# Query loads of six batches moved from the sync engine's DMA queue to GpSimd's, with a third buffer

**Chip, cores, metric.** One core of a Trainium2 chip. Times are device microseconds of a run; a profile's span, from the first to the last instruction, is one to four us shorter. PE is TensorE, DVE VectorE, ACT ScalarE, POOL GpSimd, SP the sync engine; "SPq" and "POOLq" are their queues.

## The reference

Retention over 8 batches, 8 heads, 576 tokens, head size 64, then a gated unit with a causal convolution of 5 taps. All float32 in and out.

```python
scores = scale * np.matmul(q, k.transpose(0, 1, 3, 2))
ret = scores * Dmat[None]                 # Dmat[h,i,j] = gamma_h ** (i - j) for i >= j, else 0
attn = np.matmul(ret, v)
x = attn.transpose(0, 2, 1, 3).reshape(B, S, H * D)
gate_pre = sum(conv_w[k] * xp[:, k:k + S, :] for k in range(5))    # xp: x padded in front
out = (sigmoid(gate_pre) * (x @ w_val)) @ w_out
```

## The kernel before

A batch is four chunks of 128 tokens and a tail of 64; two tails share a chunk, which makes 36 chunks. A software pipeline runs over steps t, one chunk each: keys and values are loaded six steps ahead, cast to bf16 by GpSimd, and the keys are transposed by PE. Queries come as one load of 1 MB per batch. Every second step starts a gated unit of two chunks (convolution, value product, output projection).

```python
def load_queries(b):
    t = half.tile([P, H, RQ, D], F32, name="fqb", bufs=2)
    nc.sync.dma_start(out=t.rearrange("p h r d -> p h (r d)"), in_=q[b, ...])   # 1 MB, rows of 1 KB
# ... loads ahead of the loop, sync queue:
#     k0 q(batch 0) v0 k1 v1  w_val  k2 v2  w_out  k3 v3  q(batch 1)  k4 v4 k5 v5
def prep_wo(copy, o):
    copy(wob[:, o], wof[:, o])            # output weights, f32 -> bf16, 128x512
# ...
for b in range(2, B):
    first = min(s for s in qjobs if ("batch", b, 0) in qjobs[s])
    qload.setdefault(max(0, first - LA + 2), []).append(b)     # LA = 8
# in step t, cut:
    for b in qload.get(t, []):
        load_queries(b)
    if t >= 0 and ok(t + LA - 2): load(t + LA - 2)
    if ok(t + 2): cast_v(t + 2)                                # GpSimd
    if ok(t + 3): cast_k(t + 3)                                # GpSimd from chunk 2 on
    for job in qjobs.get(t + 1, []): cast_q(job)               # GpSimd
    # ... PE: scores, values, conv, transposes, projection
    if t == 2:
        for o in range(NP):
            prep_wo(s_copy if o % 2 else v_copy, o)            # two casts on ACT, two on DVE
```

## Time and profile before

| | before |
|---|---|
| median of the first 3 runs | 177.81 us (176.45 to 177.91) |
| the profiled run | 180.25 us, which counts as slow (over 1.5% above the fastest run); span 177.4 us |
| PE / DVE / ACT / POOL busy | 86 / 66 / 50 / 46% |
| share of the DMA engines, sync queue | 90.9% |

A share of busy time says who has little slack, not who sets the end.

### The profile page before, as it was taken

Reading aid. Unit: us, or ns where it says so; the run is one execution under the profiler, and the core shown is the slowest. Engines: PE = TensorE matmul, PEld = TensorE weight load, DVE = VectorE, ACT = ScalarE, POOL = GpSimd, SP = SyncE. Lnnn points to the kernel's source line nnn. Section 1 sums busy time; section 2 is a strip of 40 time slices with the busy share of each in tenths; the row PEclk is TensorE's granted clock in tenths of the full one; section 3 lists DMA queues with packets and bytes.
Section 4 is the critical chain, followed back from the end, with each engine's and each line's share of the span. In section 5 each row is a group of like instructions: output and inputs, shape, how many; then the busy total and the mean of one; then the engine's idle time right before and its main releaser. Section 6 shows DMA issues by size and latency. Waiting matters only on the chain.

```text
span 177.4 us, 5549 instructions
## 1 busy us (share of the span) xinstructions
PE 151.7 (86%) x2273; PEld 112.2 (63%) x2273; DVE 117.7 (66%) x229; ACT 88.4 (50%) x180; POOL 81.6 (46%) x119
## 2 busy tenths in 40 slices
PE   0166359398999999999999969999999999999980
PEld 0055147247786868677786848686777868677640
DVE  6558724366867777877867747777778678876430
ACT  6351412345565565557554545655575654455231
POOL 5165135492942494631386058524775662620000
PEclk9999999969999999999999999999999999999998
DMA  5999999999999899989999979999989998853114
GB/s 126 292 280 247 220 291 211 296 294 206 266 262 256 207 271 213 251 209 235 249 247 285 287 181 245 292 207 215 288 228 224 276 251 180 203 213 123 51 68 118
DMA packets 93958, 40.20 MB, mean 227 GB/s; under 512 B 80090, under 2 KB 88302, under 8 KB 93934
## 3 DMA queue, kind: packets, MB, share of 16 engines
q1 hardware_dynamic: 93744, 39.59, 90.9%
q8 instruction: 17, 0.28, 0.7%
q10 hardware_dynamic: 190, 0.27, 0.6%
q14 instruction: 7, 0.06, 0.1%
HBM read 30.42 MB, written 9.44 MB: 225 GB/s over the span
## 4 chain that ended last, share of the span: by engine, by line
PE 74%; DMA 9%; SPq 8%; DVE 2%; POOL 2%; ACT 1%; issue 1%; ACTq 0%; DVEq 0%; POOLq 0%
PE g L391 17%; PE g L380 17%; PE g L365 12%; PE tps L222 10%; DMA fkc<-in_k_dram 9%; PE o L301 6%; PE s L260 6%; SPq L78 4%; PE st L332 4%; SPq L110 3%; PE o L284 3%; POOL kb L197 1%; DVE z L383 1%; ACT qtb L244 1%; ACT ob L394 1%
## 5 line engine op out<-in xcount | busy, mean ns | idle before, releaser
L269 DVE TENSOR_TENSOR p<-s,maskq 128x512 bf16<-128x512 f32 x64 | 43.9, 685 | 15.6 <-PE s L260 15.4
L197 POOL CAST kb<-fkc 128x512 bf16<-128x512 f32 x34 | 20.8, 611 | 50.4 <-DMA fkc<-in_k_dram 38.0
L202 POOL TENSOR_TENSOR vb<-fvc,gin 128x512 bf16<-128x512 f32 x36 | 37.6, 1044 | 12.6 <-DMA fvc<-in_v_dram 9.0
L383 DVE TENSOR_TENSOR z<-gate,g 128x512 bf16<-128x512 f32 x36 | 24.8, 688 | 20.4 <-PE g L380 20.4
L391 PE MATMUL g<-wob,z 128*128 128x512 bf16 x144 | 37.5, 389 | 0.3 <-DVE z L383 0.3
L380 PE MATMUL g<-xg,wvb 128*128 128x256 bf16 x288 | 36.9, 274 | 0.0
L394 ACT COPY ob<-g 128x512 f32<-128x512 f32 x36 | 21.1, 586 | 28.9 <-PE g L391 28.6
L373 ACT ACTIVATE gate<-g 128x512 f32<-128x512 f32 x36 | 19.5, 594 | 20.0 <-PE g L365 20.0
L380 PEld LDWEIGHTS <-wvb 128*128 128x128 bf16 x288 | 26.8, 98 | 3.5 <-issue 0.8
L343 ACT CAST sbd<-st 64x256 bf16<-64x256 f32 x48 | 17.6, 366 | 16.2 <-PE st L332 15.7
L222 PE MATMUL tps<-ident,kb 128*128 128x128 bf16 x144 | 15.1, 231 | 12.1 <-POOL kb L197 7.5
L365 PE MATMUL g<-xg,dg 64*64 64x256 bf16 x720 | 24.3, 279 | 0.0
L215 POOL CAST qb<-fqb 128x512 bf16<-128x512 f32 x30 | 18.7, 632 | 7.1 <-DMA fqb<-in_q_dram 7.1
L311 DVE TENSOR_TENSOR xg<-o,gout 128x512 bf16<-128x512 f32 x32 | 21.8, 680 | 0.0
L230 DVE COPY kt<-tps 128x512 bf16<-128x512 bf16 x36 | 15.3, 424 | 8.5 <-PE tps L222 8.2
L365 PEld LDWEIGHTS <-dg 64*64 64x64 bf16 x720 | 19.0, 109 | 2.3 <-issue 0.6
L244 ACT COPY qtb<-tps 128x512 bf16<-128x512 bf16 x27 | 15.9, 589 | 8.7 <-PE tps L222 8.7
L391 PEld LDWEIGHTS <-z 128*128 128x128 bf16 x144 | 12.9, 100 | 11.6 <-issue 1.8
L222 PEld LDWEIGHTS <-kb 128*128 128x128 bf16 x144 | 8.8, 101 | 17.5 <-POOL kb L197 8.6
L222 PEld LDWEIGHTS <-qb 128*128 128x128 bf16 x144 | 11.3, 103 | 11.6 <-POOL qb L215 4.2
L222 PE MATMUL tps<-ident,qb 128*128 128x128 bf16 x132 | 13.0, 222 | 3.3 <-DVE kt L230 1.5
L301 PE MATMUL o<-p,vb 128*64 128x128 bf16 x288 | 15.8, 235 | 0.0
(58 smaller groups left out, 123.2 us busy)
## 6 DMA issues: line engine op xcount, KB each, us to landing
fkc<-in_k_dram SPq DMA_DIRECT2D x32, 256.0 KB, 5.3
fqb<-in_q_dram SPq DMA_DIRECT2D x8, 1024.0 KB, 7.9
fvc<-in_v_dram SPq DMA_DIRECT2D x32, 256.0 KB, 5.7
out_dram<-ob SPq DMA_DIRECT2D x32, 256.0 KB, 4.3
wvf<-in_moe_w_val_dram SPq DMA_DIRECT2D x1, 1024.0 KB, 6.5
wof<-in_moe_w_out_dram SPq DMA_DIRECT2D x4, 256.0 KB, 6.2
fkc<-in_k_dram SPq DMA_DIRECT2D x8, 128.0 KB, 3.9
fqc<-in_q_dram SPq DMA_DIRECT2D x8, 128.0 KB, 4.6
```

What stands on the lines that cost most here:

```text
L197: (nc.vector if t < 2 else nc.gpsimd).tensor_copy(kb, loaded["k", *chunks[t]])
L202: nc.gpsimd.tensor_tensor(vb, loaded["v", *chunks[t]], gin[:, chunks[t][2], :].unsqueeze(2).to_broadcast([P, H, D]), op=ALU.mult)
L222: nc.tensor.transpose(ps[:, pr, :], flat[:, pr * P:(pr + 1) * P], ident)
L269: nc.vector.tensor_tensor(p, sps[t][i], m.unsqueeze(1).to_broadcast([P, NP, P]), op=ALU.mult)
L301: nc.tensor.matmul(o[r, pr, :], lhsT=vb[:, 2 * pr + i, :], rhs=pt[t, i][:, pr, :], start=(fresh and pr == 0), stop=(pr == NP - 1), skip_gr ...
L311: nc.vector.tensor_tensor(by_token(x[:, bl, :, PAD + i0:PAD + i0 + P]), ops[t].rearrange("p o (r n) -> p o n r", r=RQ), by_token(gout[:, : ...
L365: nc.tensor.matmul(g[bank][cols, pr, :], lhsT=dg[rows, blk, kk, :], rhs=xs(n, rows, blk, kk), start=(pr == 0 and kk == 0), stop=(pr == 1 a ...
L373: nc.scalar.activation(t, gps[n][i], AF.Sigmoid)
L380: nc.tensor.matmul(vps[:, j, :], lhsT=wvb[:, o, 2 * i + j, :], rhs=xs(n, slice(0, P), o, PAD), start=(j == 0 and o == 0), stop=(j == 1 and ...
L383: nc.vector.tensor_tensor(z, gsb[n][i], vps, op=ALU.mult)
L391: nc.tensor.matmul(o, lhsT=zsb[n, j // 2][:, j % 2, i * P:(i + 1) * P], rhs=wob[:, j, :], start=(j == 0), stop=(j == NP - 1))
L394: nc.scalar.copy(ob, o)
```

## The change

The intent: take the large query loads out of the line in which keys and values stand, and give them a third buffer, so that they can be issued later. Batches 0 and 1 stay on the sync queue.

```diff
         def load_queries(b):
-            t = half.tile([P, H, RQ, D], F32, name="fqb", bufs=2)
-            nc.sync.dma_start(out=t.rearrange("p h r d -> p h (r d)"),
+            t = half.tile([P, H, RQ, D], F32, name="fqb", bufs=3)
+            (nc.sync if b < 2 else nc.gpsimd).dma_start(out=t.rearrange("p h r d -> p h (r d)"),
                               in_=q[b, :, 0:RQ * P, :].rearrange("h (p r) d -> p h (r d)", r=RQ))
@@
-            qload.setdefault(max(0, first - LA + 2), []).append(b)
+            qload.setdefault(max(0, first - LA + 4), []).append(b)
```

## The prediction

> **What bounds the kernel now.** I read the page first: busy shares and the slices.
>
> ```profile
> PE 151.7 (86%) x2273; PEld 112.2 (63%) x2273; DVE 117.7 (66%) x229; ACT 88.4 (50%) x180; POOL 81.6 (46%) x119
> ...
> PE   0166359398999999999999969999999999999980
> ...
> DMA  5999999999999899989999979999989998853114
> ...
> q1 hardware_dynamic: 93744, 39.59, 90.9%
> ```
>
> A slice is 4.4 us. PE has gaps up to about 42 us and is then full to the end; the DMA engines are full from the first slice to about 150 us. Two resources are close to their limits, so the question is which of them the end follows. The view of waits answers it, for PE over the whole span, then for 42 to 168 us alone (columns: total us, times, longest):
>
> ```profile
> PE tps L222 <- POOL kb L197: 7.5, 3, 4.9
> PE tps L222 <- DVE kb L197: 4.5, 1, 4.5
> PE g L222 <- POOL qb L215: 4.0, 1, 4.0
> ```
>
> ```profile
> PE tps L222 <- POOL kb L197: 1.4, 1, 1.4
> ```
>
> From 42 us on PE waits once, for 1.4 us (at 103 us, for a key chunk that landed late). Everything else that PE loses, it loses in the first 42 us. The chain of waits names a 9 us DMA piece before 102.8 us, but the timeline of PE shows it busy until 101.7 us or so: the chain followed GpSimd's wait, of which only 1.4 us reached PE. So in steady state the end moves only with PE, and whatever delays PE once in the start is never won back: PE does its sixteen two-chunk units from 42.2 to 167.3 us back to back, 7.8 us each.
>
> In the start the largest single gap of PE that a load decides is before the transposes of key chunk 3. The timelines show it, of the load queue, of GpSimd and of PE (start us, length, what):
>
> ```profile
> 10.70 5.56 SPq L110 DMA_DIRECT2D wof<-in_moe_w_out_dram  x4
> 16.30 0.59 SPq L78 DMA_DIRECT2D fkc<-in_k_dram  x1
> 16.94 0.58 SPq L78 DMA_DIRECT2D fvc<-in_v_dram  x1
> 17.57 3.94 SPq L94 DMA_DIRECT2D fqb<-in_q_dram  x1
> 21.55 1.43 SPq L78 DMA_DIRECT2D fkc<-in_k_dram  x1
> ...
> 28.23 1.81 SPq L94 DMA_DIRECT2D fqb<-in_q_dram  x1
> ```
>
> ```profile
> 15.97 0.61 POOL L197 CAST kb<-fkc 128x512 bf16<-128x512 f32 x1
> 17.45 1.04 POOL L202 TENSOR_TENSOR vb<-fvc,gin 128x512 bf16<-128x512 f32 x1 [0.88 <-DMA fvc<-in_v_dram]
> 23.41 0.61 POOL L197 CAST kb<-fkc 128x512 bf16<-128x512 f32 x1 [4.91 <-DMA fkc<-in_k_dram]
> ```
>
> ```profile
> 18.57 0.64 PE L301 MATMUL o<-p,vb 128*64 128x128 bf16 x8
> 24.08 0.61 PE L222 MATMUL tps<-ident,kb 128*128 128x128 bf16 x4 [4.87 <-POOL kb L197]
> ```
>
> The key load of 16.30 us is chunk 3. It lands at about 23.3 us because 1 MB of output weights and what was queued before it go first; GpSimd casts it at once; PE then starts and never again waits for a load until 103 us. The query load of 28.23 us is batch 2's, the first that the change moves. It now comes behind chunks 3, 4, 5 and batch 1's queries.
>
> **What the skill says.** "DMA: Bandwidth & Descriptors", section "Issuing engines are not separate DMA queues": transfers from the sync, scalar and GpSimd queues run on the same 16 engines and interleave; another issuer saves only its issue time. The trace agrees as far as it can: there is one full resource, and the sync queue's issues take 0.4 us when there is room and up to 3.9 us when there is not. The same page, "Queues, rings and completion order": each engine takes turns between the queues that have work, packet by packet. So a GpSimd load does not stand in line behind the sync queue's; no trace here shows it yet, as nearly all goes through one queue. The same page, "Anatomy of one DMA": about 2 us fixed per GpSimd DMA, descriptor making small but variable; no duration of that is in this trace. "SBUF — State Buffer", section "SBUF: two separate sides": a copy of VectorE in a two-port mode locks GpSimd out while it makes descriptors. VectorE's large groups here (masks, gates, x, transposed keys) all read PSUM, so I expect none of it after the start.
>
> **The change part by part.** I count the main loop's steps t (one key chunk each) by the order of instructions on each engine.
>
> 1. Bytes. None are added or removed: six loads of 1 MB change their queue. Full DMA engines stay full.
>
> 2. Time of issue. The diff moves each load two steps later in program order (batch 3 from step 1 to 3, 4 from 5 to 7, 5 from 11 to 13, 6 from 15 to 17, 7 from 19 to 21). But GpSimd's program is ahead of the sync queue's, which is held by full rings and by output stores. In the timelines the sync queue issues batches 4 to 7 at 48.1, 75.3, 92.4 and 109.6 us; GpSimd begins steps 7, 13, 17 and 21 at 48.6, 72.3, 92.5 and 109.8 us. So for these four the load leaves at nearly the same moment as before. Batch 3 goes later (32.4 to about 37 us), with its first cast about 10 us after that.
>
> 3. Batch 2 is the exception. Its step is cut off at 0 both before and after, and GpSimd reaches step 0 right after its cast of key chunk 2, at 15.97 + 0.61 = 16.6 us. The third buffer is new, so nothing holds it. The load therefore leaves at 16.6 us and not at 28.2 us: 11.6 us earlier, at the same moment as key chunk 3, and beside it and not behind it.
>
> 4. What that costs key chunk 3. In the trace's DMA records those of 1,024 bytes take 54 ns in the mean; a batch of queries is 1,024 of them, 64 for each of 16 engines, so 64 x 54 ns = 3.5 us of all engines. Until chunk 3 lands, some 5.8 us of engine time remain from 17.5 us on (16.6 plus about 1 us to the first byte, an estimate from the page). With equal turns the 3.5 us of queries fit whole into that stretch. The key lands at about 23.3 + 3.5 = 26.8 us. With a slow descriptor maker that spreads the load over 10 us it would be 5.8 / (1 - 0.35) = 8.9 us after 17.5, 26.4 us, so 3.1 us late. This delay is on the path: PE sits idle for it. Later start loads do not add: chunk 4 was ready 1.6 us before PE asked for it and moves by the same 3.5 us as PE does. **+3.5 us** at the start, kept to the end.
>
> 5. What is won. At 93.75 us chunk 21's key load is issued just behind batch 6's queries and lands 8.95 us later, PE's one late wait. Beside the queries and not behind them, and with PE later by 3.5 us, it is in time. **-1.4 us.**
>
> 6. GpSimd's time for making descriptors, say d a load. Before step 17 the key cast it delays ends at 95.6 us and PE wants it at 98.6 us; step 21: 112.9 against 115.9; step 13: 75.4 against 83.2; step 7: 51.7 against 59.3; step 3: 38.3 against 43.4. Some of these casts wait for a landing first, and PE is 2 to 3.5 us later after the change, so the nearest places bear a d of about 6 to 7 us. I expect d between 1 and 6: **0 us**.
>
> 7. Removing six issues from the sync queue, in all some 12 us of its time, helps keys and values leave earlier; PE does not wait for them anyway: **0 us**.
>
> Sum: 177.8 + 3.5 - 1.4 = **179.9 us**, 1.2% slower, within 2%.
>
> **The rivals.** (a) GpSimd becomes a bound. Speaking for it: 1,024 rows per load make many descriptors, GpSimd would block in order ahead of its casts, and if d is 10 us the places of point 6 fall short by 2 to 4 us in steps 0, 3, 17 or 21. Against: GpSimd is 46% busy, and most of its idle time is waiting for landings. It would make 182 to 187 us. (b) The early load is harmless and mixing queues makes the engines more efficient, or the load's first byte is so late that chunk 3 slips by only 1 us: then the win of point 5 remains and later query waits fall away, 176.5 to 178 us. For it: between 15 and 25 us the windows show 230 to 242 GB/s, and 294 GB/s between 10 and 15 us, so small rows leave something to gain. Against: the engines' share is already over 1 in both stretches. (c) Keys and values starve in mid-kernel: a query row of 1,024 bytes takes as many turns as a key row of 256, so for some 5 us after each query load keys get a small share, and PE waits at several places by 1 to 2 us. Against: these loads had stood wholly behind the queries until now. It would make 181 to 184 us. (d) PE's clock: it ran at half speed for 3.4 us at about 37 us after the gaps of the start; a shifted start may drop or repeat such a stretch, 1.5 us to either side.
>
> **Range and chances.** Points 4 and 5 alone, with 2.5 to 4 us and 0 to 1.4 us, make 178.9 to 181.8 us; (d) and the runs' own spread of 1.4 us widen it below, (a) and (c) above: 177.4 to 183.6 us. Over 2% faster (below 174.3) would need a start that gets shorter, for which I see no mechanism: 0.03. Over 2% slower (above 181.4) takes (a), (c) or an unlucky clock: 0.25. The rest, 0.72.
>
> **What would show each step.** Right if the first query issue on GpSimd's queue stands at 16 to 18 us, the cast of key chunk 3 begins at 26 to 27 us and not at 23.4, PE's longest wait for it grows from 4.9 to about 8 us, PE's first output projection of steady state shifts by the same, and the wait at 103 us is gone. Wrong in point 3 or 4 if chunk 3's cast stays near 23.4 us; wrong in 6 if PE waits for key casts at steps 3, 13, 17 or 21 with GpSimd's queue occupied before them; wrong as a whole if PE between 45 and 168 us is no longer full, for then the end would follow the DMA engines or GpSimd.

## The result, and the profile after

The changed kernel takes **185.11 us** (184.83 to 185.59, 4 runs) against 177.86 us before (176.45 to 180.39, 4 runs): ratio 1.0438, 95% interval 1.0372 to 1.0503. It is slower by 7.3 us between the medians (7.8 us by the ratio, which leaves out the slow run), and outside the range predicted. A ratio here is the mean time of one kernel's fast runs over the mean of the other's in the same rounds, so not quite the ratio of the medians. The profiled run was fast, with a span of 183.8 us, 6.4 more than the profile before. That one is of a slow run (180.25 us). So the sums below explain the 6.4 us between these two profiles and not all of the 7.3 to 7.8 us between fast runs, and what the profile before shows, such as the stall at 103 us, may be smaller in a fast run.

The page of the changed kernel, busy shares, slices and DMA queues (packets, MB, share):

```profile
PE 153.4 (83%) x2273; PEld 113.3 (62%) x2273; DVE 122.8 (67%) x229; ACT 88.4 (48%) x180; POOL 86.9 (47%) x125
...
PE   0277092554899999999999999999999999999990
...
PEclk9999999555599999999999999999999999999999
...
q1 hardware_dynamic: 87504, 33.30, 76.7%
q0 software_dynamic: 1632, 6.29, 11.3%
```

PE is full from slice 12 on (from slice 11 before), so the middle of the kernel is not where the time went. Several of PE's first eleven slices are emptier than before (2, 5, 5, 4 and 8 in slices 7 to 11, where 9, 3, 9, 8 and 9 stood), and its clock is at half in four slices. The bytes are the same. They stand in other packets: GpSimd's loads move 6.29 MB in 1,632 packets, most of them 4,096 bytes in the trace's DMA records, where the same queries were rows of 1,024 bytes on the sync queue.

PE's waits in the changed kernel, whole span, then from 42 to 174 us:

```profile
PE tps L222 <- POOL kb L197: 9.4, 3, 4.3
```

```profile
PE g L391 <- DVE wob L190: 4.0, 1, 4.0
PE tps L222 <- DVE kt L230: 0.5, 1, 0.5
```

Waits for key casts grew from 7.5 to 9.4 us, and the one at 103 us is gone. New is a wait of 4.0 us of the output projection for VectorE's cast of the output weights. The view of that source line, before and then after (minimum, median and maximum in ns, first and last start):

```profile
L190 DVE CAST wob<-wof x2: 416/466/516, 36.0 to 36.3; 128x512 bf16<-128x512 f32 x2
```

```profile
L190 DVE CAST wob<-wof x2: 411/2962/5512, 38.3 to 43.7; 128x512 bf16<-128x512 f32 x2
```

The same instruction on the same data took 0.4 to 0.5 us before and 5.5 us now. GpSimd's timeline of the changed kernel shows what ran beside it (start, length, what):

```profile
15.95 1.06 POOL L94 DMA_DIRECT2D fqb<-in_q_dram  x1
...
22.22 0.61 POOL L197 CAST kb<-fkc 128x512 bf16<-128x512 f32 x1 [3.80 <-DMA fkc<-in_k_dram]
...
31.95 0.61 POOL L197 CAST kb<-fkc 128x512 bf16<-128x512 f32 x1 [4.32 <-DMA fkc<-in_k_dram]
...
37.29 0.92 POOL L94 DMA_DIRECT2D fqb<-in_q_dram  x1
38.23 1.05 POOL L202 TENSOR_TENSOR vb<-fvc,gin 128x512 bf16<-128x512 f32 x1
...
42.46 1.03 POOL L202 TENSOR_TENSOR vb<-fvc,gin 128x512 bf16<-128x512 f32 x1
49.42 0.61 POOL L197 CAST kb<-fkc 128x512 bf16<-128x512 f32 x1 [5.93 <-PE st L332]
```

Batch 2's load is issued at 15.95 us, batch 3's at 37.29 us, and from there GpSimd works without a gap until 43.49 us, through seven casts. VectorE's cast starts at 38.27 and ends at 43.78 us, as GpSimd falls idle. The casts of chunks 3 and 4 are the ones at 22.22 and 31.95 us: chunk 3's came at 23.41 us before, chunk 4's at 28.59:

```profile
28.59 0.61 POOL L197 CAST kb<-fkc 128x512 bf16<-128x512 f32 x1 [3.29 <-DMA fkc<-in_k_dram]
```

PE's timeline gives the sum. Before, at the transposes of chunk 4, the output projection of the first unit, and the second unit's convolution:

```profile
30.83 0.39 PE L222 MATMUL tps<-ident,kb 128*128 128x128 bf16 x4
...
37.18 3.07 PE L391 MATMUL g<-wob,z 128*128 128x512 bf16 x8
...
42.20 1.29 PE L365 MATMUL g<-xg,dg 64*64 64x256 bf16 x40
```

After:

```profile
32.62 0.55 PE L222 MATMUL tps<-ident,kb 128*128 128x128 bf16 x4 [3.86 <-POOL kb L197]
...
43.83 3.57 PE L391 MATMUL g<-wob,z 128*128 128x512 bf16 x8 [3.98 <-DVE wob L190]
...
50.17 1.29 PE L365 MATMUL g<-xg,dg 64*64 64x256 bf16 x40
```

PE is 1.8 us late at chunk 4 and 8.0 us late at the convolution. The 6.2 us between are the wait for the weights, 4.0 us, and about 2.2 us by which the same work runs longer on either side of it (2.7 - 1.8 = 0.9 ahead of the wait, 1.3 behind), where the clock is at half. From there to the end 1.6 us come back, of which the stall at 103 us is 1.4: 1.8 + 4.0 + 2.2 - 1.6 = 6.4, the difference of the spans. The windows of 5 us show the clock (last three columns: granted clock, DMA share, GB/s), before and after:

```profile
35.00:40.00 5.00, 4.74 (x36) 2.54 (x36) 2.98 (x6) 2.40 (x6) 4.38 (x7) 0.66 1.12 289
40.00:45.00 5.00, 4.48 (x89) 3.67 (x87) 2.94 (x6) 2.93 (x7) 1.70 (x3) 1.00 1.03 204
```

```profile
35.00:40.00 5.00, 3.66 (x36) 2.81 (x36) 2.50 (x3) 2.35 (x5) 4.92 (x9) 0.50 1.30 223
40.00:45.00 5.00, 1.17 (x3) 0.40 (x3) 5.00 (x4) 0.00 (x0) 3.49 (x5) 0.50 1.11 293
45.00:50.00 5.00, 4.49 (x32) 2.46 (x32) 1.40 (x4) 2.18 (x5) 0.58 (x2) 0.52 0.76 182
```

Between 40 and 45 us PE is busy for 1.17 us and VectorE for all 5.00: that is the blocked cast, counted as busy.

### The profile page after: what moved, and what is told of

It reads as the page before. It is cut to its first block, busy times and chain, and to the rows that moved or that the text cites. A ratio compares the mean times of both kernels' runs of the same rounds, so it can differ in the third digit from the quotient of the medians.

```text
span 183.8 us, 5590 instructions
## 1 busy us (share of the span) xinstructions
PE 153.4 (83%) x2273; PEld 113.3 (62%) x2273; DVE 122.8 (67%) x229; ACT 88.4 (48%) x180; POOL 86.9 (47%) x125
## 3 DMA queue, kind: packets, MB, share of 16 engines
q0 software_dynamic: 1632, 6.29, 11.3%
## 4 chain that ended last, share of the span: by engine, by line
PE 74%; SPq 10%; DMA 6%; DVE 4%; ACT 1%; issue 1%; POOL 1%; ACTq 0%; DVEq 0%; POOLq 0%
PE g L391 17%; PE g L380 16%; PE g L365 11%; PE tps L222 11%; DMA fkc<-in_k_dram 6%; PE o L301 6%; PE s L260 6%; SPq L78 5%; PE st L332 4%; DVE wob L190 3%; SPq L110 3%; PE o L284 3%; SPq L94 2%; ACT qtb L244 1%; ACT ob L394 1%
## 5 line engine op out<-in xcount | busy, mean ns | idle before, releaser
L391 PE MATMUL g<-wob,z 128*128 128x512 bf16 x144 | 38.0, 393 | 4.3 <-DVE wob L190 4.0
L365 PE MATMUL g<-xg,dg 64*64 64x256 bf16 x720 | 23.5, 273 | 0.0
L365 PEld LDWEIGHTS <-dg 64*64 64x64 bf16 x720 | 18.5, 107 | 2.1 <-issue 0.6
L222 PEld LDWEIGHTS <-qb 128*128 128x128 bf16 x144 | 12.1, 108 | 10.7 <-POOL qb L215 3.9
L222 PE MATMUL tps<-ident,qb 128*128 128x128 bf16 x132 | 14.0, 234 | 2.9 <-ACT qtb L244 1.3
```

The costliest lines, as they stand in the source:

```text
L222: nc.tensor.transpose(ps[:, pr, :], flat[:, pr * P:(pr + 1) * P], ident)
L365: nc.tensor.matmul(g[bank][cols, pr, :], lhsT=dg[rows, blk, kk, :], rhs=xs(n, rows, blk, kk), start=(pr == 0 and kk == 0), stop=(pr == 1 a ...
L391: nc.tensor.matmul(o, lhsT=zsb[n, j // 2][:, j % 2, i * P:(i + 1) * P], rhs=wob[:, j, :], start=(j == 0), stop=(j == NP - 1))
```

## The experiments

The theory: (1) batch 2's early load makes a key late at the start; (2) batch 3's load, issued just ahead of VectorE's cast, is what lets the cast wait 5 us; (3) the idle PE loses its clock, which is argued from where the stretches at half clock stand and has no run of its own; (4) the four later loads do nothing. Rivals: GpSimd's dense casts alone block the cast; the making of descriptors blocks it for a fixed time; the later loads starve keys. Every run gave a correct result. "First cast" is the longer of VectorE's two weight casts, "half clock" the length of the stretch at half speed near 40 us in the trace's clock records.

| run | median us | before, same chip | ratio (95%) | first cast us | half clock us |
|---|---|---|---|---|---|
| kernel before (profile of a slow run, 180.25) | 177.86 | - | - | 0.5 | 3.4 |
| changed kernel | 185.11 | 177.86 | 1.0438 (1.0372-1.0503) | 5.5 | 17.1 |
| wob_act | 179.15 | 177.26 | 1.0118 (1.0053-1.0184) | on ACT, 0.6 | 3.4 |
| b3_sync | 180.43 | 177.26 | 1.0189 (1.0142-1.0236) | 1.1 | 3.4 |
| b2_sync | 177.77 | 177.26 | 1.0049 (0.999-1.0107) | both in 0.82 | 0 |
| late_pool | 177.34 | 177.26 | 0.9926 (0.9846-1.0006) | 0.4 | 0 |
| b3_step4 | 179.45 | 177.27 | 1.0126 (1.0052-1.02) | 1.1 | 3.4 |
| wob_strided | 185.34 | 177.27 | 1.0497 (1.0415-1.0579) | 5.9 | 13.7 |
| b2_only | 180.49 | 177.27 | 1.0203 (1.0136-1.0269) | 0.9 | 6.8 |
| pool_gap | 179.78 | 178.16 | 1.0068 (0.9964-1.0172) | 0.5 | 6.8 |
| k3_first | 178.52 | 178.16 | 1.0042 (0.9979-1.0105) | 0.4 | 6.8 |
| k3_late_pool | 179.83 | 178.16 | 1.0126 (1.0053-1.0198) | 0.4 | 10.2 |
| probe, one run | 188.16 | - | - | 5.9 | 13.7 |
| pool_longer, one run | 186.84 | - | - | 7.7 | 13.7 |

**wob_act.** Is the blocked cast worth what the profile says?

```diff
-                    prep_wo(s_copy if o % 2 else v_copy, o)
+                    prep_wo(s_copy, o)
```

> The changed kernel, but all four casts of the output weights run on ScalarE; VectorE, whose first such cast took 5.5 us there, does none. Theory: the changed kernel's extra 7.3 us are about 4.0 us of that blocked cast, 1.8 us of key chunk 4 landing later than PE's slack covers, 2.1 us of TensorE at half clock, less 1.5 us of a stall at 103 us that is gone. If so, this takes away 4 us and part of the half-clock time: 179.5 to 181.5 us. Rival: the output projection at 43.8 us would have waited for something else at that time anyway (weights or the slot of VectorE's work), and the time stays at 184 to 185.5 us.

Measured 179.15 us, a shade below the range expected. The loss falls from 4.4% to 1.2%, with the loads as in the changed kernel: some 5.7 us ((1.0438 - 1.0118) x 177.5) hang on this one cast, its wait and the clock that PE loses in it. What is left, 2.1 us, is what the prediction had summed up for the whole change.

**b3_sync and b3_step4.** Is it the load on GpSimd, or GpSimd's dense casts?

```diff
-            (nc.sync if b < 2 else nc.gpsimd).dma_start(...)
+            (nc.sync if b in (0, 1, 3) else nc.gpsimd).dma_start(...)      # b3_sync
-            qload.setdefault(max(0, first - LA + 4), []).append(b)
+            qload.setdefault(max(0, first - LA + 4) + (b == 3), []).append(b)   # b3_step4
```

> The changed kernel, but batch 3's query load, which GpSimd issues 1 us before the blocked VectorE cast, goes out on the sync queue at the same step. Theory T1: making descriptors on GpSimd for that load holds the port that VectorE's two-port cast needs; then the cast takes 0.4 to 0.6 us here and the time is 179.5 to 181.5 us. Rival T2: GpSimd's casts, which run back to back from 37 to 43.5 us, keep VectorE out, with or without a DMA; then the cast still takes 3.5 us or more and the time stays at 183.5 to 185.5 us.

> The changed kernel, but batch 3's load is issued by GpSimd one step later (step 4), so after about 2 us more of GpSimd's casts, while VectorE's casts of the output weights stand where they did. Theory T1 (the making of descriptors keeps VectorE's cast out): the cast starts before the load is issued and takes 0.4 to 1.1 us; the time is 179 to 181 us. Rival T2 (GpSimd's back-to-back casts do): 3.5 us or more for the cast, 184 us or more.

Both times are inside the ranges given for T1 (180.43 and 179.45 us). In b3_sync the casts took longer than the 0.4 to 0.6 us that I expected of T1. The source line in b3_sync, then the timelines of VectorE and GpSimd in b3_step4:

```profile
L190 DVE CAST wob<-wof x2: 828/974/1121, 39.9 to 41.0; 128x512 bf16<-128x512 f32 x2
```

```profile
37.03 1.87 DVE L190 CAST wob<-wof 128x512 bf16<-128x512 f32 x2
```

```profile
37.81 0.80 POOL L197 CAST kb<-fkc 128x512 bf16<-128x512 f32 x1
38.56 0.81 POOL L215 CAST qb<-fqb 128x512 bf16<-128x512 f32 x1
39.32 0.92 POOL L94 DMA_DIRECT2D fqb<-in_q_dram  x1
```

GpSimd's casts stand just as dense here. Without a load ahead of them the two engines take turns: VectorE's casts take 0.8 and 1.1 us, and GpSimd's, 0.61 us elsewhere, take 0.80 and 0.81 us beside them. The skill's "SBUF — State Buffer", section "Who interferes with whom", has these turns: a copy in a two-port mode and a GpSimd instruction exclude each other for the length of one instruction. So dense casts alone (T2) cost half a microsecond each, and the load is needed for the long block.

**pool_longer, pool_gap and probe.** Is the block the making of the load's descriptors, with a length of its own, or does it last as long as GpSimd's casts follow each other?

```diff
+            if t == 5:                                         # pool_longer, behind cast_v
+                for o in range(NP):
+                    nc.gpsimd.tensor_copy(junk[:, o], wof[:, o])
+            if t == 3:                                         # pool_gap, behind load_queries
+                nc.gpsimd.tensor_copy(junk, wob[:, 2, 0:8])
+            if t >= 4:                                         # probe, at the end of the step
+                nc.vector.tensor_copy(probe[:, t % 4], wof[:, t % 4])
```

> The changed kernel with four useless casts (0.6 us each) on GpSimd behind the last of the casts that stand back to back after batch 3's load (step 5), so that GpSimd falls idle 2.4 us later. Theory T3: after a load on GpSimd its following casts leave VectorE's cast no gap until GpSimd first waits for something; then the blocked cast ends again 0.2 to 0.4 us after GpSimd's last cast, at 7.5 to 8 us length. Rival T1: the making of the load's descriptors takes some 5.5 us and the end of GpSimd's casts only happened to be near; then it stays at 5.5 us.

> The changed kernel with one tiny copy on GpSimd right after the issue of batch 3's load, which reads eight columns of the output weights that VectorE casts, so that GpSimd has to wait for that cast and is idle meanwhile. Theory T3: the first cast gets in at once, 0.4 to 1 us, GpSimd waits less than 2 us, 178.5 to 180.5 us. Rival T1: the cast stays out while the descriptors are made, 4 us or more, and GpSimd waits with it: 184 us or more.

> The changed kernel with a useless cast of 128x512 from f32 to bf16 on VectorE at the end of every step from 4 on, SBUF to SBUF, to see how long such a cast takes in each state of GpSimd. No time is expected of it (slower by the casts). Theory T1: casts that start within about 5 us of a query load's issue on GpSimd take several us, all others 0.4 to 1.1 us. Rival T2: casts are long wherever GpSimd's own casts stand back to back, load or not.

VectorE's and GpSimd's lines in pool_longer:

```profile
37.41 8.47 DVE L191 CAST wob<-wof 128x512 bf16<-128x512 f32 x2
```

```profile
43.15 2.46 POOL L449 CAST junk<-wof 128x512 bf16<-128x512 f32 x4
```

In pool_gap:

```profile
37.83 0.86 DVE L191 CAST wob<-wof 128x512 bf16<-128x512 f32 x2
```

```profile
37.21 0.92 POOL L94 DMA_DIRECT2D fqb<-in_q_dram  x1
38.76 0.18 POOL L442 COPY junk<-wob 128x8 bf16<-128x8 bf16 x1 [0.63 <-DVE wob L191]
```

With 2.4 us more of casts on GpSimd the block is longer by 2.2 us (first cast 7.73 us against 5.51). It did not end 0.2 to 0.4 us after GpSimd's last cast, as expected, but 0.5 us before that cast's end. With a gap the cast gets in at once, 0.6 us after the load's issue began, and the time is 179.78 us; a 1 MB load of 1,024 rows was being issued in all of them. That excludes a block of fixed length. Nor is the end of GpSimd's row all that can end it: in pool_longer VectorE got in ahead of the fourth useless cast (0.79 us long, the other three 0.60). By the DMA records the load itself was nearly through then (its last packet ends at 44.96 us), so a second limit by the load is not excluded. The probe agrees that a break in the row ends the block. Its first load after 50 us is issued at 54.50 us; GpSimd is idle from 56.51 us, and the probe's cast, which starts at 56.13, takes 0.67 us. Two more began beside GpSimd's first instruction behind a load, at 80.90 and 113.61 us; GpSimd then stood idle for 0.16 us, and they took 0.67 and 1.22 us. Of its 34 casts, several close behind a load, none took over 1.22 us. In the changed kernel, wob_strided and the probe's own weights' cast the block ended 0.3 us after GpSimd's unbroken row, 6.5 us after the load's issue began; in pool_longer 8.2 us after it. Why casts that follow a load leave no gap, and casts that follow casts do, no run shows.

**wob_strided.** I took a stride to be a way out of the fast form of the copy.

```diff
+            turn = lambda w: w[:, o].rearrange("p (a b) -> p b a", b=2)
+            if copy is v_copy:
+                copy(turn(wob), turn(wof))
```

> The changed kernel, but VectorE's two casts of the output weights step through their columns by two elements on both sides, so that the same 128x512 elements are read and written with a stride. If the block comes from the form of the copy[...], a strided copy takes the plain mode: about 0.6 us each, no wait, 179 to 181 us. Rival: any copy of VectorE from and to SBUF is kept out, whatever its stride: 4 us or more for the first one, 184 us or more.

185.34 us, and 5.9 us for the first cast. The second one, unblocked, took 0.44 us, nearly as fast as without a stride (0.41), so nothing shows that the stride left the fast form. The run repeats the block; it doesn't tell which form of copy is free of it.

**b2_sync and b2_only.** What is batch 2's early load worth?

```diff
-            (nc.sync if b < 2 else nc.gpsimd).dma_start(...)
+            (nc.sync if b < 3 else nc.gpsimd).dma_start(...)     # b2_sync, in the changed kernel
+            (nc.gpsimd if b == 2 else nc.sync).dma_start(...)    # b2_only, in the kernel before, bufs=3
```

> The changed kernel, but batch 2's query load stays on the sync queue, at step 0 as in the kernel before. Theory: the early load of batch 2 is what makes key chunk 4 land 3.4 us later; here its cast is back at 28 to 29 us and PE's wait before chunk 4's transposes is gone, some 1.8 us. The blocked VectorE cast may still be there: with it 182 to 184 us, without it 178 to 180. Rival: chunk 4's delay has another source (spread of DMA), then its cast stays near 32 us.

> The kernel before with three buffers and batch 2's query load alone from GpSimd, at step 0; everything else on the sync queue at its old steps. Theory: the early load costs what the run with the weights' casts on ScalarE cost over the kernel before, 1 to 3 us (178.3 to 180.3 us): one of key chunks 3 and 4 lands some 3.5 us later and PE waits for it; the VectorE casts take 0.4 to 1.1 us each. Rival: the early load is harmless by itself and the loss is all in the blocked cast: 176.5 to 178 us.

In b2_sync chunk 4's cast is back at 28.24 us, and the time, 177.77 us, is 0.2 below the range expected. PE gets to the weights' casts earlier: VectorE's two run from 35.65 to 36.47 us and are done before they can be blocked, with batch 3's load issued at 35.96 us and GpSimd's next cast at 37.05. So here the second load did no such harm without the delay that the first one brings. In b2_only chunk 4's cast begins at 31.76 us, and the time is 180.49 us, 0.2 above the range expected: early load and a longer stretch at half clock (6.8 us) cost 2% with no blocked cast.

**late_pool.** Do the four loads in the middle matter?

```diff
-            (nc.sync if b < 2 else nc.gpsimd).dma_start(...)
+            (nc.sync if b < 4 else nc.gpsimd).dma_start(...)
-            qload.setdefault(max(0, first - LA + 4), []).append(b)
+            qload.setdefault(max(0, first - LA + (2 if b < 4 else 4)), []).append(b)
```

> Batches 2 and 3 exactly as in the kernel before (sync queue, steps 0 and 1), batches 4 to 7 from GpSimd as in the changed kernel, three buffers. Theory: all the loss is in the first 50 us and the four later loads do nothing but take away the one late key at 103 us (1.4 us): 175.8 to 177.5 us, PE full from 42 us on. Rival: the later loads starve keys too (a query packet of 4,096 bytes takes a turn against a key row of 256), PE waits somewhere after 45 us: 178.5 us or more.

177.34 us against 177.26, ratio 0.9926 with 1 just inside the interval: the four loads neither cost nor win what could be told from noise. PE's waits from 52 to 170 us in late_pool (this profile's run counts as slow, 1.5% above the fastest of the kernel), and from 50 to 172 us in b2_only:

```profile
PE tps L222 <- POOL kb L197: 2.1, 3, 1.3
```

```profile
PE g L391 <- DVE z L383: 0.3, 1, 0.3
```

This corrects my reason for the vanished stall. In late_pool the later queries go round the queue and PE still waits for keys. In b2_only they stand in the old queue and PE does not wait, because PE runs later. b2_sync, whose profile is fast and whose PE is early too, still waits 0.9 us for keys there. The stall goes when PE is late; passing the queue does not remove it.

**k3_first and k3_late_pool.** Can the start be shortened by the same lever?

```diff
-        # loads of w_out (4 x 256 KB)
         load(3)
+        # loads of w_out (4 x 256 KB)
```

> The kernel before, with the 1 MB load of the output weights moved behind chunk 3's key and value loads: the same idea as the effect of batch 2's early load, with the sign turned round. Theory: what PE wins or loses at the start is kept to the end; chunk 3's key lands about 3 us earlier, chunk 4's as before, so PE gains about 2 us: 174.5 to 176 us. Rival: the gain is eaten by later waits (weights, chunk 4, the stall at 103 us growing): 176.5 to 178 us.

> The same reordering in the kernel where only batches 4 to 7 are loaded by GpSimd. Theory: the four later loads do nothing for PE, so the time is that of the other kernel with this reordering, within 1 us. Rival: with an earlier PE, later keys get tight, and loads that go round the queue cost or win 1 us or more.

k3_late_pool has late_pool's lines as well. Both missed: 178.52 and 179.83 us. In k3_first chunk 3's transposes begin at 19.82 and not at 24.08 us. Then PE waits 3.07 us for chunk 4, whose transposes begin at 30.09 us (30.83 before), and half clock lasts 6.8 us and not 3.4. A gap closed at one chunk opened at the next. k3_late_pool's four runs (179.20 to 180.84 us) all lie above k3_first's (177.81 to 178.88), as its rival had it: 1.3 us at the medians, where late_pool showed no cost. Its longer stretch at half clock (10.2 us) is over at 40.7 us, before its first load on GpSimd at 50.10 us, so these loads did not cause that part; where the 1.3 us come from stays open. None of the twelve versions beats the kernel before clear of noise.

## Why the prediction was wrong

The direction was right and the size was not: +2.1 us predicted, +7.3 measured.

- **Bound and stage.** Right. PE is full from 50 us to the end in the changed kernel, and all the loss was made before.
- **Points 1 and 2, bytes and issue times.** Right as far as late_pool shows, where batches 4 to 7 have no effect; the 1.3 us of k3_late_pool over k3_first stay unexplained.
- **Point 3, batch 2 leaves 11.6 us early.** Right: 15.95 us, at the edge of the 16 to 18 predicted, and 12.3 us earlier than before.
- **Point 4, "+3.5 us" at chunk 3.** Right in kind and about half the size at this place. I took the first byte to come 1 us after the issue. In the trace's DMA records, set to the span by chunk 0's landing, batch 2's first packet moves 6.0 us after the issue began, at 21.9 us (5.5 us and 21.5 us by the records' own times). Chunk 3's key was through by then (cast at 22.22, not 26 to 27 us) and chunk 4's stood behind: 31.95 against 28.59 us, later by 3.4 us. Chunk 4 had 1.6 us of slack, so PE lost 1.8 us. In b3_sync and b3_step4 it was chunk 3 that came late (casts at 26.62 and 25.20 us), so which of the two pays differs from run to run.
- **Point 5, "-1.4 us".** The amount is that of the two profiles, of which the one before is of a slow run; the fast profiles that still show such a wait (b2_sync, k3_first, k3_late_pool) have 0.7 to 0.9 us. The first half of its reason, that the key no longer stands behind the queries, has no support from late_pool and b2_only.
- **Point 6, "0 us" for GpSimd.** Its own part holds: an issue takes GpSimd 0.92 to 1.06 us (1 to 6 expected), and PE waits for no key cast after 42 us.
- **Point 7.** The six issues took the sync queue 9.4 us (1.81 + 2.92 + 1.60 + 0.58 + 1.29 + 1.16), not some 12; nothing hangs on it.
- **The step that failed** is in the part on the skill: "VectorE's large groups here (masks, gates, x, transposed keys) all read PSUM, so I expect none of it after the start." I went by the large groups. Two small casts of the output weights, 0.9 us in all, copy from SBUF to SBUF, and they stand at step 2, next to batch 3's load at step 3. I thought of VectorE holding up GpSimd, and what happened was the reverse. The term is missing from the sum. It measures 4.0 us of wait in the profile, and with the clock that goes with it some 5.7 us between the changed kernel and wob_act.
- **Rival (d), the clock.** I allowed 1.5 us to either side, from one stretch of 3.4 us. It was 17.1 us of half clock, about 2.2 us of PE's time more than before. The skill's "TensorE: Matmul & The Clock Gate", "Part 1: The HAM clock gate", has PE's activity judged in windows of about 3.4 us; the lengths here, 0, 3.4, 6.8, 10.2, 13.7 and 17.1 us, are multiples of that.
- **Rivals (a) and (c)**, GpSimd as the bound or starved keys in the middle: refuted by PE's waits after 50 us. **Rival (b)**, the harmless early load: refuted by b2_only, 2% slower.

With the missing term put in, the sum would have been 179.9 + 5.7 = 185.6 us; 185.11 was measured. That it comes so near is luck in part: the +3.5 us stood at the wrong chunk and was 1.8 us there, and the clock's share, a rival in the prediction, is inside the 5.7.

## What to carry to other kernels

Before a load moves to GpSimd's queue, list every VectorE copy from SBUF to SBUF near its issue, small ones first of all: put them on ScalarE, or see that they are done before the load. The block of over 5 us came only where GpSimd's own work followed the load without a break; with a break (pool_gap, probe) the cast got in. A load that leaves its queue no longer has the queue's order to protect what stood ahead of it; look for the transfer that PE needs next at that moment. And a share of busy time does not show a blocked instruction as idle: look at the longest against the shortest duration of the same form.

## What the Trainium skill lacked or had wrong

- "SBUF — State Buffer", "Who interferes with whom": it has whoever issues first hold the port pair for one instruction. That fits casts without a load (0.8 to 1.1 us). Behind a load issued by GpSimd, VectorE's cast stayed out through seven GpSimd instructions, 5.5 us, and through 7.7 us when that row was made longer. The page says that either engine can be kept out, but not for a row of the other's instructions.
- "DMA: Bandwidth & Descriptors", "Specifications": about 1 us to the first byte for GpSimd's path. In the changed kernel the first packet moved 6.0, 2.8, 2.2, 2.1, 3.0 and 2.9 us after the issue began (0.5 us less by the records' own times), with the DMA engines busy.
- The same page, "Queues, rings and completion order": it speaks of turns by packets of some 9 to 17 descriptors, not of how unequal two queues' turns can be. In the trace's DMA records batch 3's load moved as 256 packets of 4,096 bytes (1 MB) in 4.3 us, while the sync queue moved 1,097 rows of 256 bytes (0.28 MB); in the 2 us with the most packets it was 159 packets to about 120 rows.
- No page has the time that GpSimd's issue of a load of this size takes on its own timeline: 0.92 to 1.06 us for 1,024 rows of 1 KB.
